# Counting the matmuls on nothing one by one, at the cold clock's price, with new issue orders

## The chip, the cores and the metric

The kernel runs on one core of one Trainium2 chip. The metric is the device time of one execution in microseconds, the median of several runs. The core's engines are TensorE (PE, with PEld its weight loads), VectorE (DVE), ScalarE (ACT), GpSimd (POOL) and SyncE (SP); the last two also issue the transfers from and to the chip's memory. Each engine takes its instructions in the order in which they stand in its queue.

## The reference

Windowed attention with a few global tokens for 8 batches of 8 heads, then a two-layer network with a hard-swish between the layers on all 4352 tokens:

```python
s_g = scale * np.matmul(q_g, k_all.transpose(0, 1, 3, 2))        # 32 global queries against all 544 keys
out_g = np.matmul(sm(s_g), v_all)
mask = np.abs(pos[:, None] - pos[None, :]) <= 32                 # 512 local queries, a band of keys
s_ll = np.where(mask, scale * np.matmul(q_l, k_l.transpose(0, 1, 3, 2)), -1000000000.0)
s_l = np.concatenate([s_lg, s_ll], axis=-1)                      # and the 32 global keys
out_l = np.matmul(sm(s_l), np.concatenate([v_g, v_l], axis=2))
x = np.concatenate([out_g, out_l], axis=2).transpose(0, 2, 1, 3).reshape(B * S, H * D)
h = x @ w_in                                                     # 512 -> 2048
out = (h * np.clip(h + 3.0, 0.0, 6.0) / 6.0) @ w_out             # 2048 -> 512
```

Head width is 64, so a token has 512 features. Inputs and output are float32; the kernel multiplies in float16.

## The kernel before

**Work.** For each batch b the 512 local tokens are taken in four blocks j of 128. A step (b, j) has a score on TensorE (`pe` in `local_step`, L673, 64 small matmuls into the one PSUM tile `s`), a masked maximum for each head on VectorE (L699), an exponential for each head on ScalarE (L710), a scaling on VectorE (L726, L732), a transpose of the weights (for the first three batches on TensorE, L743, with a copy out of PSUM at L396 or L398; from batch 3 on by a DMA on SyncE, L755), and the product with v (L764, L767). From the seventh step on, the product of two steps before is joined to the score as one step of TensorE. The global queries of a batch follow (L813 to L881). Then comes the network for that batch: `first` (L895 matmul, L902 ScalarE, L906 VectorE) and `second` (L918, then a copy and a store on SyncE, L935).

**The start.** Batch 0's blocks 0 and 1 come as float32 on SyncE's queue (`load_single`, L508: q and k of a block; `load_halo`, L519: 32 more keys) and are turned by TensorE against an identity in float32 (`turn_single`, L530). All other loads stand on GpSimd's queue (L475): `natg` (global queries and keys), `nat` (q and k of a block), `ve` (values), `vgz`, `win` and `wout`. The identity is made by VectorE (memset), GpSimd (L434) and VectorE again (L437, the cast to float32). The masks go the same way (L406, L410 and L412, then copies at L417 to L419). The first score needs the turned q, k, halo and global keys (`turn_g`, L638), each copied out of PSUM.

**The order of the work.** Nothing schedules itself. The program numbers its steps (`Op`, 2139 of them); `ORDER` at L16 holds, for each engine, the numbers in the order of its queue; some copies may go to ScalarE or VectorE, and the lists say to which. `Plan.lay` (L209) replays these lists with a cost for each step and a model of the transfers, and so finds the order in which the instructions are written out and which buffer each step takes.

**Matmuls on nothing.** TensorE's clock is low until the engine has been busy for a while, so the plan has it multiply a tile of zeros (`idle`, L440 and L1045, 128x128 by 128x512) in gaps, up to a given step of batch 1. How many of them stand ahead of a step is worked out in `lay` from the planned gap: its length less 150 ns, divided by one fill. A fill is priced `FILL` = 216 ns, twice that if the step starts before `COLD` = 5000 ns; the price goes by the start of the step behind the gap, and holds for the whole gap. The same `COLD` doubles the duration of steps that start before it. The numbers stand at L187; all times there are the plan's own clock.

**Steps named later.** 12 and 14 turn q and k of block 0, 17 the halo, 55 the global keys, 65 is the first score; 21 and 23 turn q and k of block 1, 61 block 2; 2 is the identity's cast, 9 the mask copies, 5 a second clearing of buffers (the second run of L445 to L449); 13 and 18 copy the turned q and the halo, 56 the keys; 26 loads v_g of batch 0, 47 to 50 copy it into `vgz`; 25 loads the first global keys; 36 to 39 load w_in.

Of the kernel before, what the change touches and what calls it, by code (L numbers as in the profile page):

```python
# [65 lines left out]
    """,  # L66
    "DVE": """
# [114 lines left out]
class Plan:  # L182
# [4 lines left out]
    COLD, FILL = 5000.0, 216.0  # L187
# [895 lines left out]
```

## Time and profile before

| what | us |
|---|---|
| median of 3 runs | 326.71 |
| lowest and highest | 323.97, 328.09 |
| the profiled execution's own time | 323.58 |
| its span, from the first to the last instruction | 321.8 |
| TensorE's last matmul | 318.5 |

A profile row has the start, the length, the engine, the line, the operation, the tiles (written <- read) and the count; in brackets stands how long the engine had been idle and what ended that. Consecutive instructions of a kind are merged into a row. Lengths of matmuls overlap, since they are pipelined: the pace is the distance between starts. "DMA to landing" is the time from a transfer's issue to the signal that it is there. The page's own account of the slices, for orientation: TensorE is at 9 tenths or more from the second slice to the last but one.

### The profile page before, as it was taken

To read this page: it belongs to the slowest core of one execution; us is meant where nothing else is said; L and a number is where in the kernel's file an instruction comes from. 1 tells how busy PE (TensorE), PEld (TensorE's weight loads), DVE (VectorE), ACT (ScalarE), POOL (GpSimd) and SP (SyncE) were. 2 spreads that over 40 slices of the span, in tenths; PEclk is the share of its full clock that TensorE was granted. 3 is DMA by queue.
4 is the path that set the end of the run, shared out by engine and by line. 5 is a ranking of instruction groups with operands and counts; after the bars stand their busy time and mean duration, and the time that the engine had idled before them with its cause. 6 is when DMAs were issued, how large, how long until landed. Compare 5 with 4: busy or idle time off the path is not lost.

```text
span 321.8 us, 9641 instructions
## 1 busy us (share of the span) xinstructions
PE 315.2 (98%) x3606; PEld 181.2 (56%) x3606; DVE 264.7 (82%) x968; ACT 237.0 (74%) x760; POOL 121.5 (38%) x167
## 2 busy tenths in 40 slices
PE   8999999999999999999999999999999999999995
PEld 3567876668865545444544554445444445446653
DVE  4799999989987998879998998989989885475500
ACT  2899999989995798787967897787878853474201
POOL 7968866999188274127065160300000000000000
PEclk9999999999999999999999999999999999999999
DMA  9999999999999999999996999984594218100033
GB/s 160 169 189 168 150 222 171 145 189 153 181 167 188 170 140 152 176 198 143 196 161 111 210 131 191 162 135 105 98 188 113 41 34 191 65 2 0 2 113 115
DMA packets 173614, 45.03 MB, mean 140 GB/s; under 512 B 164096, under 2 KB 168448, under 8 KB 173568
## 3 DMA queue, kind: packets, MB, share of 16 engines
q0 software_dynamic: 108800, 17.28, 73.1%
q1 hardware_dynamic: 64768, 27.14, 41.0%
q8 instruction: 28, 0.46, 0.6%
q14 instruction: 18, 0.15, 0.1%
HBM read 35.65 MB, written 8.91 MB: 138 GB/s over the span
## 4 chain that ended last, share of the span: by engine, by line
PE 84%; DVE 5%; POOL 4%; ACT 2%; DMA 2%; issue 1%; POOLq 0%; DVEq 0%; ACTq 0%
PE m L918 36%; PE m L895 33%; PE s L673 4%; PE a L764 3%; PE a L767 3%; DMA nat<-in_q_l_dram 2%; PE m L743 2%; DVE gs L906 1%; PE a L872 1%; POOL ve L475 1%; DVE sm L699 1%; PE m L623 1%; POOL nat L475 1%; PE s L813 1%; ACT sm L710 1%
## 5 line engine op out<-in xcount | busy, mean ns | idle before, releaser
L918 PE MATMUL m<-wout,gs 128*128 128x512 f16 (+1 forms) x560 | 127.8, 373 | 0.0
L895 PE MATMUL m<-xt,win 128*128 128x512 f16 (+2 forms) x704 | 119.8, 321 | 0.4 <-DVE et L398 0.2
L710 ACT ACTIVATE sm<-sm,stat 128x160 f32<-128x160 f32 x256 | 106.9, 422 | 12.1 <-DVE stat L699 11.8
L906 DVE SCALAR_TENSOR_TENSOR gs<-t,m 128x512 f16<-128x512 f32 x136 | 91.6, 682 | 17.4 <-ACT t L902 16.5
L895 PEld LDWEIGHTS <-win 128*128 128x128 f16 x768 | 69.0, 98 | 48.3 <-issue 1.0
L902 ACT ACTIVATE t<-m 128x512 f32<-128x512 f32 x136 | 79.5, 592 | 22.3 <-PE m L895 21.8
L918 PEld LDWEIGHTS <-gs 128*128 128x128 f16 x560 | 53.1, 98 | 54.7 <-issue 1.4
L699 DVE CUSTOM_DVE_ANT_0 sm<-s,mask 128x160 f32<-128x160 f32 x256 | 69.1, 316 | 0.7 <-PE s L673 0.6
L710 ACT ACTIVATION_READ_ACCUMULATOR sm<-sm,stat 128x1 f32 x256 | 49.3, 193 | 0.0
L726 DVE TENSOR_TENSOR pn<-sm,stat 128x512 f16<-128x512 f32 x64 | 43.7, 687 | 1.0
L475 POOL DMA_DIRECT2D ve<-in_v_l_dram x40 | 32.8, 828 | 14.6 <-PE a L872 11.6
L475 POOL DMA_DIRECT2D nat<-in_q_l_dram x30 | 27.0, 906 | 26.8 <-DMA qk<-nat 22.5
L475 POOL DMA_DIRECT2D nat<-in_k_l_dram x30 | 27.2, 907 | 4.0 <-DMA vgz<-in_v_g_dram 1.4
L396 ACT CAST xt<-a 128x512 f16<-128x512 f32 x27 | 15.7, 581 | 17.1 <-PE a L767 10.1
L475 POOL DMA_DIRECT2D vgz<-in_v_g_dram x28 | 15.8, 570 | 32.8 <-PE a L767 32.8
L396 ACT COPY ot<-m 128x512 f32<-128x512 f32 (+1 forms) x21 | 11.9, 568 | 19.4 <-PE m L918 13.8
L699 DVE DVE_READ_ACCUMULATOR2_ANT stat<- 128x1 f32 x256 | 20.8, 81 | 0.0
L673 PEld LDWEIGHTS <-qk 64*64 64x64 f16 x1024 | 13.6, 107 | 12.2 <-issue 11.1
L398 DVE COPY ot<-m 128x512 f32<-128x512 f32 (+1 forms) x14 | 9.3, 667 | 11.4 <-PE m L918 11.4
L673 PE MATMUL s<-qk 64*64 64x128 f16 x512 | 16.8, 224 | 1.0 <-ACT qk L396 0.5
L1045 PE MATMUL a<-idle 128*128 128x512 f16 x51 | 15.3, 433 | 1.2 <-DVE idle L440 1.2
L828 DVE TENSOR_REDUCE stat<-s 128x1 f32<-128x544 f32 x16 | 11.5, 717 | 4.4 <-PE s L813 3.7
(78 smaller groups left out, 265.0 us busy)
## 6 DMA issues: line engine op xcount, KB each, us to landing
out_dram<-ot SPq DMA_DIRECT2D x31, 256.0 KB, 3.6
nat<-in_q_l_dram POOLq DMA_DIRECT2D x30, 128.0 KB, 5.7
nat<-in_k_l_dram POOLq DMA_DIRECT2D x30, 128.0 KB, 6.0
st<-ve SPq DMA_DIRECT2D x14, 256.0 KB, 4.2
ve<-in_v_l_dram POOLq DMA_DIRECT2D x24, 128.0 KB, 5.1
win<-in_moe_w_in_dram POOLq DMA_DIRECT2D x4, 512.0 KB, 7.2
wout<-in_moe_w_out_dram POOLq DMA_DIRECT2D x4, 512.0 KB, 9.6
ve<-in_v_l_dram POOLq DMA_DIRECT2D x8, 96.0 KB, 5.2
```

Of the source, the lines that this page charges most:

```text
L396: nc.scalar.copy(out=out, in_=in_)
L475: nc.gpsimd.dma_start(out=dst(op), in_=src)
L673: nc.tensor.matmul(out=out[q, P:KW] if n == G else out[q, 0:P], lhsT=qk[r][rows, 0, p, UQ + j * P + u * QP:UQ + j * P + (u + 1) * QP], rhs ...
L699: nc.vector.tensor_tensor_reduce(out=sm[sm_op.slot][:, h, :], in0=head(psS[s.slot], h), in1=m, scale=-scale, scalar=3.0e38, op0=ALU.add, o ...
L710: nc.scalar.activation(out=sm[sm_op.slot][:, h, :], in_=sm[sm_op.slot][:, h, :], func=EXP, scale=-1.0, bias=stat[stat_op.slot][:, 0, h:h + 1],
L726: nc.vector.tensor_tensor(out=pn[pn_op.slot][:, h0:h1, :], in0=sm[sm_op.slot][:, h0:h1, 0:P], in1=stat[stat_op.slot][:, 2, h0:h1].unsqueez ...
L828: nc.vector.tensor_reduce(out=w[:, 0, 0:1], in_=at, axis=AX, op=ALU.max)
L895: nc.tensor.matmul(out=psM[op.slot][:, i * n:(i + 1) * n], lhsT=w_in_t[:, m, (c + i) * P:(c + i + 1) * P], rhs=x()[:, m, t0:t0 + n], start ...
L902: nc.scalar.activation(out=t1[to.slot], in_=psM[f.slot], func=RELU, bias=0.5, scale=1.0 / 6.0)
L906: nc.vector.scalar_tensor_tensor(out=gs[set_.slot][:, c:c + k, t0:t0 + n], in0=t1[to.slot].rearrange("f (k t) -> f k t", k=k), scalar=1.0, ...
L918: nc.tensor.matmul(out=psM[(f or op).slot][:, a * n:(a + 1) * n], lhsT=gs[set_.slot][:, c, t0:t0 + P], rhs=w_out_t[:, c, a * n:(a + 1) * n ...
L1045: order = plan.fill(plan.lay(av_last[1, 0]), lambda ring, i: lambda: nc.tensor.matmul(out=spare[ring][i], lhsT=idle[:, 0:P], rhs=idle))
```

## The change

The counting of fills in `lay` becomes a loop that places them one by one. Each is priced by its own start, not by the start of the step behind the gap, and `COLD` moves from 5000 to 5400:

```diff
-    COLD, FILL = 5000.0, 216.0
+    COLD, FILL = 5400.0, 216.0
...
             if o.eng == "PE":
-                one = self.FILL * (2 if s < self.COLD else 1)
                 if o is until:
                     filled = False
                 if filled and where[0] <= at:
-                    o.idle, o.where = max(int((s - at - 150) / one), 0), where[1:]
+                    o.where = where[1:]
+                    while True:
+                        at += self.FILL * (2 if at < self.COLD else 1)
+                        if at > s - 150:
+                            break
+                        o.idle += 1
+                        full.append((at, self.WHOLE))
                     count += 2 * o.idle
-                    full += [(at + one * (i + 1), self.WHOLE) for i in range(o.idle)]
                 full = [x for x in full if x[0] > s - self.WINDOW]
```

All five lists of `ORDER` are new. The beginnings:

```diff
     "PE": """
-        12 55 14 17 65 23 21 61 99 93 90 63 131 95 163 391 124 127 399 129 156 387 403 57 235 159 195 237 161
+        12 55 14 17 65 21 23 61 99 93 90 63 131 95 163 124 127 391 399 129 156 387 57 403 237 159 195 235 161
...
     "ACT": """
-        6 13 15 69 75 71 73 83 81 77 79 24 48 49 52 50 107 109 115 94 117 103 105 113 111 143 135 96 97 139 386
+        6 15 77 71 69 75 73 79 81 83 24 48 52 105 107 109 113 103 94 115 111 117 137 149 96 97 135 147 145 139
...
     "DVE": """
-        3 4 0 5 7 9 2 56 18 60 66 67 68 74 70 78 84 82 72 80 98 76 85 22 86 62 87 47 88 89 100 101 106 108 110
+        7 0 3 4 2 9 5 56 13 18 60 49 50 47 66 67 76 70 74 68 72 78 98 84 80 22 85 82 86 62 87 89 88 100 101 104
...
     "POOL": """
-        25 1 29 8 30 28 26 31 32 33 42 34 27 37 230 35 229 39 36 215 40 219 216 41 217 218 220 487 38 228 223
+        25 26 1 8 29 30 28 31 32 33 34 27 487 35 37 229 39 41 228 36 40 42 215 217 218 216 219 220 38 489 221
...
     "SP": """
-        10 11 16 20 19 234 233 501 471 502 770 773 478 774 771 457 772 1022 769 464 750 801 729 1024 1021 828
+        10 11 16 19 20 234 233 502 457 464 501 478 772 774 471 771 770 773 736 750 769 1022 801 1021 828 1023
```

In the built program this comes to 41 fills in place of 56: 7 in place of 19 ahead of the first real step of TensorE, and 34 in place of 37 behind it. Of the steps that keep their engine, 26 of SyncE's 110 keep their place in its queue, 16 of GpSimd's 162, 214 of VectorE's 818, 168 of ScalarE's 644 and 232 of TensorE's 380, where none moves by more than 8 places. Fourteen copies move from VectorE to ScalarE and eleven the other way, step 13 and two of the v_g copies (49, 50) among them. What is computed is the same.

176 rows, old and new, of the table ORDER are left out of this document.

## The prediction

> **What bounds the kernel now.** I read the page's head first, then a table of stages, and then the first ten microseconds in order of time, engine by engine.
>
> ```profile
> span 321.8 us, 9641 instructions
> PE 315.2 (98%) x3606; PEld 181.2 (56%) x3606; DVE 264.7 (82%) x968; ACT 237.0 (74%) x760; POOL 121.5 (38%) x167
> ```
>
> TensorE looks full for 98% of the span. But the matmuls on nothing (L1045) count as busy, so the next table cuts the span into stages, and the one behind it shows those matmuls alone.
>
> ```profile
> 0.00:10.00 10.00, 8.80 (x68) 4.42 (x68) 4.07 (x31) 2.90 (x5) 8.31 (x17) 1.00 1.31 160
> 10.00:50.00 40.00, 38.06 (x668) 29.09 (x658) 39.07 (x163) 38.66 (x128) 30.76 (x42) 1.00 1.72 182
> 50.00:250.00 200.00, 199.89 (x2398) 110.97 (x2394) 184.01 (x695) 165.50 (x558) 82.46 (x110) 1.00 1.35 158
> ```
>
> ```profile
> 0.00:10.00 10.00, 6.94 (x20) 2.42 (x20) 1.00 1.31 160
> 10.00:50.00 40.00, 9.58 (x36) 3.18 (x36) 1.00 1.72 182
> 50.00:322.00 272.00, 0.00 (x0) 0.00 (x0) 1.00 1.06 133
> ```
>
> The columns of the first are the stage, its length and the busy time of PE, PEld, DVE, ACT and POOL; the second has PE and PEld. There are three regimes. From 50 us on TensorE is full of real work (199.89 of 200): nothing there waits long, and the end comes when that work is done. From 10 to 50 us VectorE (39.07 of 40) and ScalarE (38.66) set the pace, and TensorE pads its gaps with 36 matmuls on nothing. Before 10 us VectorE did only 4.07 us of work: all are waiting for the first score. So the start is the only place with time to be had from the fills, and what the start loses moves everything behind it.
>
> ```profile
> 1.20 6.55 PE L1045 MATMUL a<-idle 128*128 128x512 f16 x19 [1.20 <-DVE idle L440]
> 7.58 0.60 PE L530 MATMUL m<-ident,single 128*128 128x128 f32 x4
> 8.02 0.39 PE L638 MATMUL m<-ident,natg 128*128 128x128 f16 x4
> 8.78 0.43 PE L530 MATMUL m<-ident,t 32*128 32x32 f32 x4
> 9.52 0.31 PE L673 MATMUL s<-qk 64*64 64x128 f16 x4
> ```
>
> ```profile
> 5.44 0.15 PEld L1045 LDWEIGHTS <-idle 128*128 128x128 f16 x1 [0.28 <-issue]
> 5.85 1.39 PEld L1045 LDWEIGHTS <-idle 128*128 128x128 f16 x7 [0.27 <-issue]
> ```
>
> TensorE's order opens with 19 fills; the first real step (the turn of q, L530) starts only when they are done, at 7.58, without any wait of its own. The weight loads tell the clock (its column in the tables above says 1.00 throughout): up to 5.85 a fill took 0.41 to 0.43 us, the seven behind it some 0.2 us each. So the planner of before, which priced all 19 at 0.216, put 12 cold ones at half their cost: 12 x 0.21 = 2.5 us of fills too many.
>
> Was the data there earlier?
>
> ```profile
> L508 SPq DMA_DIRECT2D single<-in_q_l_dram x1: 452/452/452, 0.7 to 0.7; - x1
> DMA to landing us min/median/max: 3.1/3.1/3.1
> L475 POOL DMA_DIRECT2D natg<-in_k_g_dram x1: 717/717/717, 1.7 to 1.7; - x1
> DMA to landing us min/median/max: 3.9/3.9/3.9
> L519 SPq DMA_DIRECT2D t<-in_k_l_dram x1: 707/707/707, 1.9 to 1.9; - x1
> DMA to landing us min/median/max: 4.0/4.0/4.0
> 2.53 0.31 POOL L434 TENSOR_SCALAR_AFFINE_SELECT ident<-ident 128x128 f16<-128x128 f16 x1
> 4.37 0.22 DVE L417 COPY mask<-mask 64x128 f32<-64x128 f32 x1 [0.96 <-POOL mask L412]
> 5.31 0.19 DVE L437 CAST ident<-ident 128x128 f32<-128x128 f16 x1
> 8.44 0.22 DVE L398 COPY gt<-m 128x128 f16<-128x128 f16 x1 [2.94 <-PE m L638]
> 9.24 0.29 DVE L398 CAST qk<-m 128x128 f16<-128x128 f32 x1 [0.58 <-PE m L530]
> 10.17 0.32 DVE L699 CUSTOM_DVE_ANT_0 sm<-s,mask 128x160 f32<-128x160 f32 x1 [0.64 <-PE s L673]
> ```
>
> Yes: q landed at 0.74 + 3.1 = 3.8, the global keys at 1.7 + 3.9 = 5.6, the halo at 1.9 + 4.0 = 5.9. The identity in f32 was ready at 5.5 only because its cast stood behind the mask copies. TensorE's own fills held the start back by about 2 us.
>
> **The change part by part.** *Fills ahead of the first turn, 19 to 7.* They now end at 1.20 + 7 x 0.43 = 4.2 us. The identity no longer stands behind the mask: on GpSimd one load (v_g) goes ahead of L434, at most the 0.72 us that the k_g issue takes, so 2.84 + 0.72 = 3.6, and the cast makes 3.8. The q turn can start at 4.2. The other three turns took 8.02 to 9.21 = 1.19 us and cannot start before the keys' landing, 5.6 to 5.9 (their load waits for a memset that now stands third): 7.0 at the latest, while the clock is up. VectorE's queue ends later than that:
>
> ```profile
> 2.17 0.07 DVE L445 MEMSET qk<- 128x16 uint32 x1
> 3.22 0.19 DVE L406 MEMSET mask<- 128x160 f32 x1
> 12.82 0.66 DVE L398 CAST qk<-m 128x512 f16<-128x512 f32 x1
> ```
>
> Mask copies from 4.37 to 5.31 (they wait for GpSimd, whose load ahead of them is now shorter); the second clearing, put behind them, 3.22 - 2.17 = 1.05, to 6.4; the key copy 0.22; the q copy 0.66, moved over from ScalarE, to 7.2; the halo copy 0.29, to 7.5. The first score starts at about 7.5 against 9.52: **2.0 us earlier**. Three copies of v_g (moved ahead of the first softmax) lie in the 0.65 us between 9.52 and 10.17, in which VectorE waits for the score anyway.
>
> *Fills behind the first score, 37 to 34.* Three fewer, 3 x 0.22 = 0.65 us less of gap in the plan. VectorE and ScalarE set that stage, not TensorE, and their work is the same; I take nothing of it, and keep 0 to -0.65.
>
> *Loads, on GpSimd's queue.* Moving everything forward uses up their lead.
>
> ```profile
> 4.29 0.90 POOL L475 DMA_DIRECT2D nat<-in_k_l_dram  x1
> DMA to landing us min/median/max: 5.7/5.7/5.7
> 12.48 0.61 PE L623 MATMUL m<-ident,nat 128*128 128x128 f16 x8
> L475 POOL DMA_DIRECT2D win<-in_moe_w_in_dram x1: 765/765/765, 14.7 to 14.7; - x1
> DMA to landing us min/median/max: 9.1/9.1/9.1
> 27.17 2.16 PE L895 MATMUL m<-xt,win 128*128 128x128 f16 x32
> ```
>
> Block 2's keys landed at 10.0 and were turned at 12.48, a lead of 2.5; v_g's issue now stands ahead (0.7), so 1.8 are left for a gain of 2.0. The first group of w_in landed at 23.8 and was used at 27.17, a lead of 3.3; its place moves back by one small load (0.7), which leaves 2.6. So the 2.0 us just pass under the loads. TensorE takes its steps in order, so where a landing is late the whole queue behind it waits. I put 0 to +1.0 on this, and take 0.
>
> *The searched orders of the rest.* Nearly every queue is permuted: on SyncE 26 of 110 steps keep their place, on TensorE 232 of 380, none further off than 8 places. From 50 us on TensorE had 0.1 us of visible wait in 200, so little is to be gained. I cannot work a loss out from here; I take 0, and bound it by the scatter of the kernel before, 323.97 to 328.09: -2 to +2.
>
> Sum on the profiled execution: 323.58 - 2.0 = 321.6. That execution lies below the median, 326.71; the same gain on the median gives **324.7**.
>
> [...] In the trace the clock rose between 5.44 and 5.85, with TensorE filled without a gap since 1.20. In the new order TensorE runs dry from about 5.1, when the q turn ends (0.44 us from 7.58 to 8.02 at the full clock, twice that below it), to 5.6 or later. [...]
>
> **The rivals.** (a) *The clock stays low for longer,* since the fills that fed it are gone. For: the dry stretch above. Against: after it TensorE is busy again. Priced from rows: the three turns (1.19) and the first score (9.52 to 10.17, 0.65) would take up to twice their time, 1.8 us: gain 0.2, 326.5. [...] (b) *The start is hidden anyway:* the loads or the two busy engines give back the 2 us before 50 us. For: the leads of 1.8 and 2.6 are thin. Against: VectorE stood idle for 6 of the first 10 us and for 0.9 of the 40 behind. Time: 326.7. (c) *SyncE's queue blocks,* which ends on the other side.
>
> ```profile
> SPq L755 <- DVE pn L732: 29.1, 8, 10.8
> et<-pn SPq DMA_TRANSPOSE x20, 3.8
> ```
>
> From block 3 on the turned weights come by 20 transposes on SyncE, in order with stores and strips. If a store that still waits stands ahead of one of them, the attention product, and with it all of TensorE's queue, waits. SyncE itself waited up to 10.8 us there without harm, since the score runs two steps ahead; that speaks against it. One such wait is worth up to the 3.8 us of a landing; from one on the gain is gone, and with two the kernel takes 324.7 + 7.6 = 332, with three 336. (d) *More than I count:* the 0.65 of the later fills and 2 us by better orders: 322.
>
> **How the numbers follow.** Forecast 0.50 (324.7); (a) 0.12; (b) 0.17; (c) 0.12; (d) 0.09. Two per cent, about what a measurement of this kernel can tell from no change, is 6.5 us: under 320.2 or over 333.2. The forecast, (a) and (b) are within; of (c) I give 0.08 to slower; of (d) 0.06 to faster, where the medians scatter as well: 0.06, 0.86, 0.08. The range runs from 321.0 (the forecast with its bounds of -0.65 and -2 and most of (d)) to 329.5 ((a) and (b) with +2, and one block of (c)).
>
> **What would show it.** Right: 7 fills to 4.2 us, the first L530 there, the first score near 7.5, the first L699 near 8.2, and TensorE full by about 46 to 48 us. Weight loads 0.43 apart beyond 6 us show (a). L623 or L895 waiting for a DMA before 30 us shows (b). A wait of L764 for a DMA after 100 us shows (c). I am wrong if the first score comes at 7.5 and the end does not follow, or if the identity or a landing holds the first turns to 7 us.

## The result and the profile after

| | before | after |
|---|---|---|
| median of 22 runs, us | 324.25 | 327.22 |
| lowest and highest | 322.79, 328.83 | 324.33, 330.38 |
| after / before, 95% interval | | 1.0083 [1.006, 1.0107] |
| the profiled execution's own time, its span | 323.58, 321.8 | 324.33, 322.6 |

The kernel became 0.8% slower, where 0.6% faster had been forecast. (Ratios here and below leave out executions more than 1.5% above the fastest of the same kernel.) Two things are to be kept in mind. The three runs from which the forecast started had a median of 326.71; with 22 runs the kernel before stands at 324.25. And the execution profiled after is the shortest of its 22, so its trace shows less loss than the typical run has.

The head of the page, and the table of stages (stage, length, busy us of PE, PEld, DVE, ACT and POOL):

```profile
span 322.6 us, 9631 instructions
PE 313.0 (97%) x3591; PEld 180.1 (56%) x3591; DVE 263.7 (82%) x965; ACT 239.7 (74%) x763; POOL 121.0 (38%) x167
```

```profile
0.00:10.00 10.00, 8.29 (x66) 4.72 (x67) 6.84 (x44) 2.78 (x7) 8.08 (x16) 1.00 1.34 160
10.00:50.00 40.00, 36.04 (x653) 28.02 (x651) 39.11 (x154) 38.42 (x129) 30.50 (x42) 1.00 1.72 182
50.00:250.00 200.00, 199.37 (x2386) 110.36 (x2380) 181.20 (x684) 166.28 (x554) 82.45 (x110) 1.00 1.41 157
```

VectorE has 6.84 us of work before 10 us in place of 4.07: the start did move forward. TensorE is busy for 36.04 of the 40 us behind, with 38.06 before: it has fewer fills there (29 in place of 36), and it waits more. From 50 us on it is a little less full than it was, 199.37 against 199.89.

The start in order of time, first TensorE (start, length, engine, line, operation, tiles, count, and in brackets the idle time and what ended it), then VectorE:

```profile
1.19 3.17 PE L1049 MATMUL a<-idle 128*128 128x512 f16 x7 [1.19 <-DVE idle L444]
4.19 1.09 PE L534 MATMUL m<-ident,single 128*128 128x128 f32 x4
5.80 0.61 PE L642 MATMUL m<-ident,natg 128*128 128x128 f16 x4 [0.52 <-DMA natg<-in_k_g_dram]
7.19 0.43 PE L534 MATMUL m<-ident,t 32*128 32x32 f32 x4
7.93 0.32 PE L677 MATMUL s<-qk 64*64 64x128 f16 x4
```

```profile
3.66 0.29 DVE L441 CAST ident<-ident 128x128 f32<-128x128 f16 x1 [1.26 <-POOL ident L438]
7.66 0.29 DVE L402 CAST qk<-m 128x128 f16<-128x128 f32 x1 [0.39 <-PE m L534]
7.98 1.49 DVE L402 COPY vgz<-ve 32x128 f16<-32x128 f16 x3
8.94 0.53 DVE L703 CUSTOM_DVE_ANT_0 sm<-s,mask 128x160 f32<-128x160 f32 x1
```

Line numbers stand four higher than before. Seven fills, the first turn at 4.19, 0.52 us dry until the global keys land, the first score at 7.93: 1.6 us earlier than the 9.52 of before. The turns were slow: from 5.80 to 7.62 they took 1.82 us, where they took 1.19 before at the full clock, which came only at 7.1 here. In a kernel below whose clock was up at 3.9 the same turns took 1.2 and the score came at 7.33. The three copies of v_g hold VectorE from 7.98 to 8.94, so the first softmax begins 1.2 us earlier (8.94 against 10.17).

Where the 1.6 us went is read from the first score matmul (L673, after L677) of six steps, and from the end of TensorE's last matmul. By each of these points TensorE has done the same work in every kernel, fills aside. The score of (1,1) is no such point: the new order puts a turn of keys (L627, 0.5 us) ahead of it. The table gives, for the profiled executions, how much later these came than in the kernel before, in us (negative is earlier), and beside it when the clock rose, from the trace's clock records. The lower rows are experiments that follow.

| | clock up at | (0,0) | (0,1) | (1,2) | (1,3) | (2,2) | (6,0) | last matmul |
|---|---|---|---|---|---|---|---|---|
| before, at us | 5.8 | 9.52 | 14.46 | 49.40 | 55.67 | 77.50 | 196.43 | 318.45 |
| after | 7.1 | -1.6 | -1.0 | -0.5 | -0.1 | -0.2 | +1.0 | +0.9 |
| after, a second execution | 13.2 | -1.1 | +0.5 | +0.6 | +0.7 | +0.6 | +1.7 | +1.6 |
| after, load 224 earlier | 4.0 | -2.2 | -1.9 | -2.2 | -2.1 | -2.2 | -0.6 | -0.6 |
| new counting alone | 5.7 | -1.9 | -1.9 | -1.5 | +3.9 | +3.8 | +3.8 | +3.8 |
| counting, 12 fills over the wait | 5.8 | -1.9 | -1.9 | +0.7 | +0.7 | +0.6 | +0.6 | +0.6 |
| counting, loads in order of need | 5.3 | -2.0 | -2.0 | -2.0 | -1.7 | -1.6 | -1.0 | -1.0 |
| the same with new engine orders | 3.9 | -2.2 | -1.8 | -1.7 | -1.6 | -1.7 | -0.3 | +0.8 |

The 12 fills stand ahead of the score of (1,2), so they are in its figure.

The rows for (6,0), the kernel before first and then the kernel after:

```profile
196.43 0.25 PE L673 MATMUL s<-qk 64*64 64x128 f16 x4
```

```profile
197.39 0.25 PE L677 MATMUL s<-qk 64*64 64x128 f16 x4
```

So the gain is lost in three places: between (0,0) and (1,2), 1.1 us; around the joined step (1,2) near 50 us, 0.4 here, which shows best in the experiments; and between (2,2) and (6,0), 1.1 us. In the first place the new orders brought waits of TensorE that were not there before, from the table of its waits (total, times, longest):

```profile
PE s L677 <- DVE stat L725: 1.1, 1, 1.1
PE m L627 <- DVE gs L910: 0.6, 1, 0.6
```

The first stands ahead of the score of (0,1), which waits for VectorE (before, it waited 0.5 us for ScalarE). Between (0,0) and (0,1) two things come together. With the old engine lists at most 0.1 us is lost there. With the new ones 0.4 us is lost where the clock was up by 4.0, 0.6 where it rose at 7.1, and 1.6 where it rose at 13.2; in that last execution TensorE was itself the slower one, and the wait for VectorE was gone. From (0,1) to (1,2) the rows lose at most 0.5 us with either lists, the 12 fills aside.

The second place is a strip: SyncE copies a piece of batch 1's values into `st` (L582, after L586) as soon as GpSimd's load 224 has brought them, and the product with v (L764, after L768) of the joined step (1,2) waits for it. Its issue on SyncE and its landing, from the view by source line, and its use, from the timeline, first before and then after:

```profile
L582 SPq DMA_DIRECT2D st<-ve x1: 462/462/462, 42.2 to 42.2; - x1
DMA to landing us min/median/max: 6.8/6.8/6.8
```

```profile
50.01 0.29 PE L764 MATMUL a<-et,st 128*64 128x64 f16 x8
```

```profile
L586 SPq DMA_DIRECT2D st<-ve x1: 461/461/461, 42.5 to 42.5; - x1
DMA to landing us min/median/max: 7.2/7.2/7.2
```

```profile
49.82 0.32 PE L768 MATMUL a<-et,st 128*64 128x64 f16 x8 [0.17 <-DMA st<-ve]
```

Before it landed at 42.2 + 6.8 = 49.0 and was used at 50.01, a lead of 1.0 us: less than the two leads (2.5 and 3.3) that the prediction checked, and less than the 2.0 us by which all should move forward. After it landed at 49.7 and TensorE waited for it. The wait here is short because this execution had only 0.5 us of its lead left. And the fills end at just this step, so that TensorE has nothing to do in a wait here; with counting alone, below, the clock fell in such a wait, of 2.44 us.

The third place shows in part as waits, from the table of TensorE's waits behind 60 us, where the kernel before has none:

```profile
PE s L677 <- ACT sg L840: 0.3, 1, 0.3
PE a L876 <- ACT sm L714: 0.3, 1, 0.3
```

### The profile page after: what moved, and what is told of

Same layout as the page of the kernel before. It is cut to its first block, busy times and chain, and to the rows that moved or that the text cites. A ratio compares the mean times of both kernels' runs of the same rounds, so it can differ in the third digit from the quotient of the medians.

```text
span 322.6 us, 9631 instructions
## 1 busy us (share of the span) xinstructions
PE 313.0 (97%) x3591; PEld 180.1 (56%) x3591; DVE 263.7 (82%) x965; ACT 239.7 (74%) x763; POOL 121.0 (38%) x167
## 3 DMA queue, kind: packets, MB, share of 16 engines
q1 hardware_dynamic: 64768, 27.14, 41.7%
## 4 chain that ended last, share of the span: by engine, by line
PE 82%; DMA 9%; POOL 5%; ACT 2%; issue 1%; DVE 1%; POOLq 0%
PE m L922 36%; PE m L899 32%; DMA win<-in_moe_w_in_dram 5%; PE s L677 4%; PE a L768 3%; PE a L771 3%; DMA st<-ve 2%; DMA ve<-in_v_l_dram 2%; POOL ve L479 2%; POOL nat L479 1%; PE a L876 1%; PE m L747 1%; PE s L817 1%; PE m L627 1%; ACT sm L714 1%
## 5 line engine op out<-in xcount | busy, mean ns | idle before, releaser
L400 ACT CAST xt<-a 128x512 f16<-128x512 f32 x30 | 17.4, 580 | 18.7 <-PE a L771 10.5
L400 ACT COPY ot<-m 128x512 f32<-128x512 f32 (+1 forms) x25 | 14.1, 564 | 11.6 <-PE m L922 11.0
L677 PEld LDWEIGHTS <-qk 64*64 64x64 f16 x1024 | 13.5, 108 | 12.5 <-issue 11.4
L677 PE MATMUL s<-qk 64*64 64x128 f16 x512 | 16.5, 224 | 2.0 <-DVE stat L725 1.1
L725 DVE RECIPROCAL stat<-stat 128x4 f32<-128x4 f32 x64 | 10.5, 171 | 9.4 <-ACT sm L714 8.9
L677 PE MATMUL s<-gt,qk 64*64 64x32 f16 x512 | 14.5, 176 | 0.0
```

The costliest lines, as they stand in the source:

```text
L400: nc.scalar.copy(out=out, in_=in_)
L677: nc.tensor.matmul(out=out[q, P:KW] if n == G else out[q, 0:P], lhsT=qk[r][rows, 0, p, UQ + j * P + u * QP:UQ + j * P + (u + 1) * QP], rhs ...
L725: nc.vector.reciprocal(out=stat[stat_op.slot][:, 2, h0:h1], in_=stat[stat_op.slot][:, 1, h0:h1])
```

## The experiments

In each, "counting" is the new loop with `COLD` 5400, and the ratio is to the kernel before on the same chip. The lists of `ORDER` are those of before unless the edit says otherwise. "Low clock" counts executions whose mean granted clock was under 0.998. The profile of counting alone, with two stretches of 3.41 us at half speed (50.0 to 56.9), has a mean of 0.990; a fall of one such stretch (a "window" in the expectations) comes to 0.995, an estimate from that. The mean does not take in the start: it is 1.000 in the profile of the run that follows, with the clock up only at 13.2 us.

**The kernel after once more**, with no edit.

> The changed kernel as it is, for a second profile and the granted clock of each execution. Its first profile was one of its fastest executions (324.33 against a median of 327.22). Theory A, the new orders leave loads and copies no lead, so that TensorE stalls between 20 and 50 us by an amount that differs between executions: a typical profile shows the first score near 8 us as before, and the lead over the old kernel (1.2 us at step 0,3) gone or turned into 2 to 3 us of loss by step 1,2, with TensorE's gaps ended by DMA or by copies that waited for loads. Theory B, with fewer fills TensorE's clock falls again for a window or two: executions with a mean clock of 0.995 or 0.99 are 2 to 3 us slower than those at 1.000, and the kernel before shows none such. Ratio to the kernel before: 1.006 to 1.011 under both.

Median 325.62, ratio 1.0057 [1.0034, 1.0081], low clock in 3 of 10. The profiled execution (325.11) shows what the first did not. TensorE's timeline:

```profile
5.91 0.61 PE L642 MATMUL m<-ident,natg 128*128 128x128 f16 x4 [0.69 <-DMA natg<-in_k_g_dram]
8.40 0.32 PE L677 MATMUL s<-qk 64*64 64x128 f16 x4
10.06 1.91 PE L1049 MATMUL a<-idle 128*128 128x512 f16 x4
```

Four fills at 10.06 last 1.91 us: they start 0.43 apart. By the trace's clock records the clock rose only at 13.2 us, where it rose at 5.8 before and at 7.1 in the first execution of after. The score of (0,1) came 0.5 us later than before. That is rival (a), the clock that stays low longer; of its loss 0.5 us falls ahead of the first score (8.40 against 7.93) and 1.6 us behind it, between (0,0) and (0,1).

**Counting alone** (46 fills, 9 ahead of the first turn).

```diff
-    COLD, FILL = 5000.0, 216.0
+    COLD, FILL = 5400.0, 216.0
...
+                    while True:
+                        at += self.FILL * (2 if at < self.COLD else 1)
+                        if at > s - 150:
+                            break
+                        o.idle += 1
```

> The counting and COLD of the change, the five issue orders of the kernel before: 46 fills, 9 ahead of the first turn. The q turn should start at 5.5 (the identity's cast, which this order leaves behind the mask), the first score at about 7.5 to 8. Theory A (the orders cost, the fills gain): ratio 0.992 to 0.998, 1 to 2.5 us faster than the kernel before, clock 1.000. Theory B (the missing fills cost through the clock): mean clocks under 1.000 in a third of the executions, ratio 1.000 to 1.010. Theory C, the start is hidden by the loads: ratio 0.998 to 1.002 with the first score early all the same.

326.02, ratio 1.0039 [1.0007, 1.007], low clock in 7 of 12; the five at full clock have a median of 323.98, the seven others 326.32. With the old queues the first score comes at 7.59, and a lead of 1.5 us reaches the joined step. There it meets the strip (timeline of TensorE, then the table of stages, whose column before the last two is the granted clock):

```profile
48.35 0.32 PE L768 MATMUL a<-et,ve 128*64 128x64 f16 x8
51.10 0.43 PE L768 MATMUL a<-et,st 128*64 128x64 f16 x8 [2.44 <-DMA st<-ve]
51.86 3.62 PE L922 MATMUL m<-wout,gs 128*128 128x512 f16 x8
```

```profile
48.00:50.00 2.00, 0.66 (x40) 0.50 (x37) 1.97 (x9) 2.00 (x9) 2.00 (x3) 1.00 1.50 254
50.00:52.00 2.00, 0.90 (x13) 0.87 (x14) 2.00 (x8) 1.29 (x7) 0.79 (x2) 0.51 1.44 197
52.00:54.00 2.00, 2.00 (x7) 0.62 (x6) 0.19 (x2) 1.41 (x5) 1.95 (x3) 0.50 2.21 161
54.00:56.00 2.00, 2.00 (x11) 1.17 (x10) 0.00 (x0) 0.00 (x0) 0.94 (x2) 0.50 2.42 157
56.00:58.00 2.00, 2.00 (x14) 1.21 (x12) 1.18 (x5) 0.42 (x2) 1.86 (x3) 0.78 2.13 136
```

TensorE waits 2.44 us, the clock goes to half from 50.0 to 56.9, and matmuls on w_out last 0.43 in place of 0.22 us. The lead of 1.5 becomes a lag of 3.9, which then stands to the end. So a late strip costs twice: the wait, and the clock that it lets fall.

The lead of 1.0 us explains only 0.5 of this wait. The rest is that the strip itself came later than in the kernel before, at 44.7 + 6.3 = 51.0 and not at 49.0. In the profile of the run with 12 more fills, whose loads stand in the same order (on another chip), it came at 41.7 + 7.0 = 48.7 (first this run, then that one):

```profile
L586 SPq DMA_DIRECT2D st<-ve x1: 462/462/462, 44.7 to 44.7; - x1
DMA to landing us min/median/max: 6.3/6.3/6.3
```

```profile
L589 SPq DMA_DIRECT2D st<-ve x1: 461/461/461, 41.7 to 41.7; - x1
DMA to landing us min/median/max: 7.0/7.0/7.0
```

So the landing moved by over 2 us between two executions with the same list, by a cause that stays open, and a lead read from one profile is not a fixed number.

**The new orders alone** (the old counting, all five new lists: 42 fills, 7 ahead). The edit is to the kernel after:

```diff
-    COLD, FILL = 5400.0, 216.0
+    COLD, FILL = 5000.0, 216.0
...
+                one = self.FILL * (2 if s < self.COLD else 1)
...
+                    o.idle, o.where = max(int((s - at - 150) / one), 0), where[1:]
```

> The five new orders with the old counting and COLD 5000; since the plan starts the first turn before 5 us here, the old counting also gives 7 fills there, 42 in all. Theory A: the whole loss comes with the orders, ratio 1.006 to 1.011, like the changed kernel. Theory B: the same, since the fills are nearly the same, with clocks under 1.000 in a third of the executions. If the ratio is at or under 1.002 then neither the orders nor the number of fills costs the time, but the few places where the two countings differ.

326.31, ratio 1.0053 [1.0026, 1.008], low clock in 6 of 12. The old counting on the new lists also gives 7 fills ahead, so the start is as early; its profile shows the strip's wait (2.8 us) and a fall of the clock. Counting and orders cannot be told apart by this run alone: either brings the start forward into the same strip.

**Counting, with the new lists of GpSimd and SyncE and the old ones of the engines.**

```diff
     "POOL": """
-        25 1 29 8 30 28 26 31 32 33 42 34 27 37 230 35 229 39 36 215 40 219 216 41 217 218 220 487 38 228 223
+        25 26 1 8 29 30 28 31 32 33 34 27 487 35 37 229 39 41 228 36 40 42 215 217 218 216 219 220 38 489 221
...
     "SP": """
-        10 11 16 20 19 234 233 501 471 502 770 773 478 774 771 457 772 1022 769 464 750 801 729 1024 1021 828
+        10 11 16 19 20 234 233 502 457 464 501 478 772 774 471 771 770 773 736 750 769 1022 801 1021 828 1023
...
```

> The changed counting, the old orders of TensorE, ScalarE and VectorE, the new orders of the two queues that issue transfers (GpSimd and SyncE); 46 fills, 9 ahead of the first turn. Theory A1, the loads' new order is what costs: ratio 1.003 to 1.011, and TensorE's lead after the first score is lost before 50 us as in the changed kernel. Theory A2, the engines' new orders cost and the queues' do not: ratio 0.992 to 0.999, near that of the fills alone.

328.21, ratio 1.0129 [1.0089, 1.0169], low clock in 5 of 6. TensorE's timeline has one long wait behind the start:

```profile
115.27 0.32 PE L768 MATMUL a<-et,ve 128*64 128x64 f16 x8 [3.29 <-DMA et<-pn]
```

A fall of the clock at 116.1 stands behind it. It looks like rival (c), but SyncE's queue was not blocked: the transpose was issued at 106.84, as soon as VectorE had written its input (106.40 + 0.42), and took 8.4 us to land (VectorE's timeline, then the transpose by its source line):

```profile
106.40 0.42 DVE L736 TENSOR_TENSOR pn<-sm,stat 128x256 f16<-128x256 f32 x1
```

```profile
L759 SPq DMA_TRANSPOSE et<-pn x1: 2376/2376/2376, 106.8 to 106.8; - x1
DMA to landing us min/median/max: 8.4/8.4/8.4
```

In the kernel before the same transpose was issued at 107.8 and landed in 4.6 us. The kernel after, which has the new engine orders beside these queues, waits 0.59 us for a transpose at 173.47 in its second profile and not at all in its first. What makes the landing slow, and which of the two queues has a part in it, was not tried.

**Counting, with load 224 ahead of 43, 222 and 232.**

```diff
-        489 227 226 488 221 225 43 222 232 224 45 231 498 44 490 481 46 479 482 500 480 485 492 483 761 484 486
+        489 227 226 488 221 225 224 43 222 232 45 231 498 44 490 481 46 479 482 500 480 485 492 483 761 484 486
```

> The fills-only kernel (changed counting, old orders) with one load moved: step 224, the first values of batch 1, directly behind 225 on GpSimd's queue, ahead of a w_out group, a half of q and k, and a small load. Step 224 is the last that batch 1's second strip transfer on SyncE waits for, and in the fills-only profile TensorE stood 2.4 us at that strip and its clock fell for 6.8 us right there. Theory D (the strip's landing is the true bound of the start, and the wait for it also costs the clock): the strip is issued near 42.5 in place of 44.7, lands before 49, TensorE's wait there is under 0.5 us, the clock stays at 1.000 in most executions, and the start's gain of 1.5 to 2 us reaches the end: ratio 0.992 to 0.997. Theory B (fewer fills cost the clock wherever TensorE is not padded, strip or no strip): ratio 1.000 to 1.006, mean clocks under 0.996 in a third of the executions as before.

324.34, ratio 1.0008 [0.9978, 1.0039], low clock in 1 of 12. The strip's wait is gone, and another stands in its place:

```profile
46.13 0.40 PE L626 MATMUL m<-ident,nat 128*128 128x128 f16 x4 [2.46 <-DMA nat<-in_k_l_dram]
```

That is load 222, which was moved back by the one that was moved forward: one load moved alone only hands the wait on.

**The kernel after with load 224 earlier.** The edit is to the kernel after:

```diff
-        226 223 222 227 230 225 45 232 491 231 224 479 43 44 490 46 488 481 482 480 492 483 496 484 494 1001
+        226 223 222 227 230 225 224 45 232 491 231 479 43 44 490 46 488 481 482 480 492 483 496 484 494 1001
```

> The changed kernel with step 224 moved ahead, directly behind 225 (ahead of a w_out group and three small loads). Theory D: the wait at the strip goes and with it most low clocks near 50 us; what is left is the start's gain of 1.2 less about 1 us that the new engine orders lose between batches 2 and 6: ratio 0.997 to 1.002. Theory B: 1.004 to 1.010, as the changed kernel.

Ratio 1.0018 [0.997, 1.0066], low clock in 5 of 12, over all executions a median of 327.76 (322.83 to 333.66): inconclusive as a time. Its profile, of its shortest execution, keeps 2.2 us at (2,2), with the clock up at 4.0, and has 0.6 of it left at (6,0) and at the last matmul: the third loss, without the second.

**The kernel before with load 224 later.** Nothing of the change is in it.

```diff
-        489 227 226 488 221 225 43 222 232 224 45 231 498 44 490 481 46 479 482 500 480 485 492 483 761 484 486
+        489 227 226 488 221 225 43 222 232 45 231 498 44 224 490 481 46 479 482 500 480 485 492 483 761 484 486
```

> The kernel before with step 224 moved back, behind 45, 231, 498 and 44: the strip is issued some 2.5 to 3 us later (45 in place of 42.2) and lands near 52, while TensorE wants it at 50. All fills and engine orders are those of before. Theory D: TensorE waits 1.5 to 2.5 us there, the clock falls in a part of the executions, ratio 1.004 to 1.014. Theory B: no more than the wait itself, ratio 1.003 to 1.007, and clocks stay at 1.000 since the fills are all there.

331.68, ratio 1.022 [1.0165, 1.0275], low clock in 6 of 6:

```profile
56.33 0.42 PE L763 MATMUL a<-et,st 128*64 128x64 f16 x8 [6.24 <-DMA st<-ve]
```

From 0.6 earlier the kernel goes to 7.8 us later at this one step, and stays there. The wait is far longer than expected, since the strip was issued only at 49.8 and not at 45. This one move costs 2.2%.

**Counting, with 12 fills ahead of the joined step.** The loads stay as they are, and fills take the place of the wait.

```diff
                 if o is until:
                     filled = False
+                    if where[0] <= at:
+                        o.where, o.idle = where[1:], 12
+                        count += 24
```

> The fills-only kernel with 12 more matmuls on nothing directly ahead of the step that waits for the strip (1,2), 2.6 us of them, so that TensorE is busy while the strip is under way. The wait is not shortened, but the clock has no reason to fall there. If the wait alone costs: the same ratio as fills-only, 1.002 to 1.007, or 0.1 to 0.3% more. If the clock's fall is the larger part (theory D's second half): mean clocks of 0.998 to 1.000, time 323.5 to 325, ratio 0.998 to 1.003, with a narrower scatter than the 322.7 to 327.8 of fills-only.

324.86, ratio 1.0016 [0.9984, 1.0048], low clock in 0 of 12, where it was 7 of 12 without these fills. So the falls went with TensorE standing still there, and matmuls on nothing over the wait prevented them. The 12 take 2.75 us themselves, so no lead is left.

**Counting, with the 14 loads around 224 in the order in which they are needed.**

```diff
-        38 228 223 489 227 226 488 221 225 43 222 232 224 45
+        38 228 223 227 226 221 225 222 224 232 43 489 488 45
```

> The fills-only kernel with fourteen loads of GpSimd's queue in another order, the fills unchanged (46, in the same places): the values of batch 1 (226, 225, 224) and its last half of q and k (222) go ahead, one w_out group (43) and two small loads for batch 2 (489, 488) behind them. Moving 224 alone only handed TensorE's wait on, from the strip to the turn of block (1,3), 2.5 us at the half of k that had come later. Theory D2 (the start is bound by the order of the loads that are needed by 50 us, and it can be ordered): no wait over 0.6 us between 40 and 52 us, clock 1.000 in nearly all executions, the 1.5 to 2 us reach the end: ratio 0.993 to 0.997. Theory C2 (it is bound by the transfers' own rate, whatever their order): a wait of 1 to 3 us turns up at another load, ratio 0.999 to 1.005.

**322.64 (321.71 to 323.83), ratio 0.9951 [0.9928, 0.9974], low clock in 0 of 12**: faster than both kernels. The strip is issued 4.7 us earlier than before, lands at 37.5 + 7.7 = 45.2, and its use at 47.97 waits for nothing (the strip by its source line, then the timeline):

```profile
L585 SPq DMA_DIRECT2D st<-ve x1: 462/462/462, 37.5 to 37.5; - x1
DMA to landing us min/median/max: 7.7/7.7/7.7
```

```profile
47.97 0.29 PE L767 MATMUL a<-et,st 128*64 128x64 f16 x8
195.40 0.25 PE L676 MATMUL s<-qk 64*64 64x128 f16 x4
```

The last row is (6,0), at 196.43 before. Of the 2.0 us at the start 1.0 reaches it: 0.4 goes to a wait for w_out at 52.4, and 0.5 to a transpose at 111.

**The kernel before with the same 14 loads.**

> The kernel before with the same fourteen loads reordered, fills and engine orders as they were (19 fills at the start). It tells whether the load order gains by itself. Theory D2: the kernel before did not wait at these loads, so it has nothing to gain: ratio 0.998 to 1.001, with fewer low clocks than the kernel before beside it. If it gains as much as the run with the new counting, the fills had no part in it.

323.77, ratio 0.9988 [0.9963, 1.0012], low clock in 0 of 12. Alone, the loads bring nothing that can be measured; what is gained is the early start, and the loads let it through.

**Counting and loads in order, with the identity's cast moved up in VectorE's queue** (45 fills, 7 ahead). The edit is to the kernel of 322.64:

```diff
-        3 4 0 5 7 9 2 56 18
+        3 4 0 7 2 5 9 56 18
```

> The run with the new counting and the reordered loads, and the identity's cast (step 2) on VectorE ahead of the second clearing and the mask copies; 7 fills ahead of the first turn in place of 9. The first turn starts near 4.2 in place of 5.4, but the keys land at 5.6 to 5.9, so the first score gains 0 to 0.6 us over that run: ratio 0.991 to 0.997 under theory D2, and no better than that run if the keys' and the halo's landing set the first score. The gap between the first turn and the keys can put the clock's rise off (to 9 us or later, as in the second profile of the changed kernel, where it rose at 13.2): then the first score comes 0.4 us later, not earlier.

322.62, ratio 0.996 [0.9935, 0.9984], low clock in 0 of 12. The cast is no longer late, but the keys' landing ends the wait, and the first score comes at 7.72 in place of 7.55. The clock's rise was not put off to 9 us: it came by 7.1. No gain from it.

**Counting, with the loads in order and the new lists of TensorE, VectorE and ScalarE** (load 26 second and step 8 ahead of 29, as in the kernel after; SyncE's list of before; 37 fills in place of 46). The edit is again to the kernel of 322.64:

```diff
     "PE": """
-        12 55 14 17 65 23 21 61 99 93 90 63 131 95 163 391 124 127 399 129 156 387 403 57 235 159 195 237 161
+        12 55 14 17 65 21 23 61 99 93 90 63 131 95 163 124 127 391 399 129 156 387 57 403 237 159 195 235 161
...
     "POOL": """
-        25 1 29 8 30 28 26 31 32 33
+        25 26 1 8 29 30 28 31 32 33
```

> The changed counting and the new orders of TensorE, ScalarE and VectorE, with SyncE's old queue and GpSimd's old queue (its fourteen loads reordered as in the run that beat both, and v_g of batch 0 in second place, which the new VectorE order needs); 37 fills. In every profile with the new engine orders the scores lost 1.1 to 1.7 us against the old kernel between batches 2 and 6, in those with the old engine orders and queues 0 to 0.6. Theory E1, the engines' orders lose it: the lead of 1.5 to 2 us at batch 2 shrinks by 1.1 to 1.7 us here too, ratio 0.998 to 1.002. Theory E2, the new queues of SyncE and GpSimd lose it: the lead stays, ratio 0.993 to 0.997.

325.36, ratio 1.0042 [1.0018, 1.0066], low clock in 3 of 12. Against 0.9951 with the old lists that is 0.9 points, 2.7 us between the medians; the nine fills fewer are part of this difference. The profile has lost 1.4 us from (2,2) to (6,0) and 2.4 to the last matmul, where the old lists lose 0.6 to either. Waits that the kernel before did not have, from TensorE's timeline:

```profile
96.61 0.25 PE L677 MATMUL s<-qk 64*64 64x128 f16 x4 [0.32 <-ACT sg L840]
160.20 0.74 PE L876 MATMUL a<-eg,ve 128*128 128x64 f16 x20 [0.88 <-DMA eg<-pg]
279.24 1.02 PE L899 MATMUL m<-xt,win 128*128 128x512 f16 x4 [0.97 <-DVE ot L402]
```

Together they are 2.2 us, each at another place. Which exchange in which list makes them was not tried.

## Why the prediction was wrong

**The fills ahead of the first turn: right in kind, 0.4 us too much.** Seven fills to 4.2 us, the turn there, the identity at 3.9 and a dry stretch until the keys land were all forecast. The score came at 7.93 and not 7.5, a gain of 1.6: the three turns had been priced at 1.19 us "while the clock is up", and took 1.82 since it rose only at 7.1. The forecast of the first softmax at 8.2 failed by more: the copies of v_g were said to lie in 0.65 us of waiting, but that wait was for the very score that had moved. They took 0.96 us of VectorE's queue. And a start with fewer fills hangs on when the clock rises: with the new lists it decides whether 1.9 us or nothing is left at (0,1).

**The later fills: taken at nothing.** TensorE's fills were not what set the pace there, and no run shows a gain from fewer. That they also guard the clock was not costed: beyond the joined step there are none, and a wait of 2.4 us there let the clock fall for two stretches (counting alone); with 12 fills over it no execution of 12 had a fall.

**Where the forecast's 2.0 us went in the kernel after.** In the two profiles, from the table of steps: 0.4 and 0.9 us short at the first score, 0.6 and 1.6 to (0,1), 0.5 and 0.1 to (1,2), 0.4 and 0.1 to (1,3), a gain of 0.1 in both to (2,2), and 1.1 and 1.0 behind it: 2.9 and 3.6 in all, from 2.0 earlier to 0.9 and 1.6 later. So three steps of the prediction failed: the gain at the start, which took the clock to be up in time; the loads, taken at 0; and the searched orders, taken at 0. What took the 0.5 us ahead of (1,2) is not shown.

**"So the 2.0 us just pass under the loads": the step that fails for the counting by itself.** It checked two leads, block 2's keys and w_in. The shortest lead on the way was batch 1's strip, 1.0 us, which is not a load of GpSimd at all but a copy on SyncE behind one. The 0 to +1.0 put on this term was far too small, since it priced neither a landing that comes 2 us later in another execution nor what a wait does to the clock: counting alone swung by 5.4 us at this place. Three runs show it: late in the kernel before, the load costs 2.2%; with fills over the wait, the clock stays up; with the loads in order, the early start becomes a gain.

**The searched orders: the second term that failed.** From bounds of -2 to +2 the value 0 was taken; measured, the three engines' lists, with the 37 fills that they leave, cost 0.9 points, 2.7 us between the medians, against the lists of before on nearly the same loads (1.7 us between the two profiled executions, 322.56 and 324.24). TensorE's 0.1 us of wait in 200 was read as "little is to be gained"; it also meant that another order could hardly win there, and could lose. In sum, against the best kernel (0.9951): the loads of before instead of the ordered ones cost 0.9 points (1.0039), the new engine orders 0.9 (1.0042), and the kernel after, with new orders and its own unordered loads, 1.3 or 1.1 (1.0083, and 1.0057 measured again).

**The rivals.** (a) came true in both profiled executions of after, in part with the clock up at 7.1 us and more than in full with 13.2; what sets the moment of the rise is not shown. The clock records show only that the full-clock stretches have a measure in common: they are 317.44 us long in the kernel before and in the first execution of after, and 44.37, 47.79, 109.23 and 269.65 us in others of these runs, that is 93, 13, 14, 32 and 79 times 3.413. (b), that the loads give the start back before 50 us, is nearest to what happened, but in its own price it ended at no change: it had no fall of the clock. That its 326.7 lies close to the measured 327.22 is luck: it is the median of three runs of a kernel that stands at 324.25 in 22. (c), a transpose held up in SyncE's queue, stands behind none of the long waits: the wait of 3.29 us was for a slow landing.

**What the prediction's marks said.** "I am wrong if the first score comes at 7.5 and the end does not follow" is what occurred, with 7.93. The mark for (b) looked for a wait before 30 us, at L623 or L895; the strip's stands at 50, at L764. The mark for (c), L764 waiting for a DMA after 100 us, appeared in the second profile of after (0.59 us at 173.47) without (c): that transpose was issued at 167.34, when its input had been ready for 0.06 us.

**What stays open.** The kernel after at full clock has a median of 326.98 (14 of 22 runs), 2.65 us above its profiled execution; the eight runs with a low clock have 327.99, so falls of the clock behind the start are the smaller part. Only profiled executions can be read, so how the typical one splits between a late rise at the start, short waits at the strip and the engines' orders is not shown. What brings the clock's rise from 7.1 to 13.2 in the same kernel is open too. The kernel before had a low clock in 10 of 102 executions beside the experiments, with no cause that these runs show.

## What to carry to other kernels

Before pulling a start forward, list the lead of every landing on the critical path behind it, transfers chained to other transfers included; what goes beyond the smallest lead turns into a wait there, unless the loads are reordered with it. Read each lead from several executions: here one landing moved by over 2 us between two executions with nothing changed ahead of it. Where TensorE's own order changes too, compare only points by which it has done the same work. A wait of 2 to 3 us in a kernel bound by TensorE is to be priced with the clock that it may let fall: with counting alone 6.8 us at half speed came with a wait of 2.44. Matmuls on nothing over it kept the clock up here, with a fall in 0 of 12 executions in place of 7 of 12. Where TensorE already waits for nothing, a newly searched order of the other engines is a risk to be measured by itself.

## What the runs showed of the hardware

With counting alone the clock went to half at 50.0 us, 1.4 us after the matmul that ended at 48.67 and within a wait of 2.44 us, and came back at 56.9, two stretches of 3.41 us later. A wait of 2.46 us in another kernel (load 222, at 43.7 to 46.1) left the clock at 1.000. So the length of these two waits does not tell whether the clock falls. Nor does TensorE's busy time in a stretch of 3.413 us, counted on from the clock's rise, in these runs: with counting alone the clock fell behind a stretch with 1.80 us of it (46.63 to 50.04), but stretches with 1.93 in the kernel that waited for load 222 (44.66 to 48.07) and with 1.56 at the end of the kernel of 322.64 (315.87 to 319.28) left the clock up.

The rise at the start is as uncertain. TensorE's fills begin at 1.20 us before and at 1.19 after, but the time from there to the rise is not fixed: in 13 of the 14 profiled executions the clock rose between 3.9 and 7.1 us, and in one at 13.2, though that one's wait for the keys, 0.69 us, was hardly longer than the 0.52 of the same kernel's other execution. The granted clock in the stage tables reads 1.00 in all of them, so the start has to be read from the pace of the fills: 0.43 us below the full clock, 0.22 at it.
